# Gated recurrence and maxout feed-forward on one core: two single units first, a split last store, six more transposes by transfer, and a reordered plan

## The chip, the core and the metric

The kernel runs on one core of one Trainium2 chip. The metric is device time in microseconds (us), from the start to the end of one launch. Times are medians over runs; one execution was also taken by the hardware profiler, and its span (first to last instruction) and its own time are given where they are used.

## What is computed

Two stages follow each other. The first is a gated linear recurrence over 768 steps for 4 batches of 8 heads with 48 channels; the second is a feed-forward layer with three gates of which the largest is taken:

```python
for t in range(S):
    state = alpha[:, :, t, :, None] * state + np.einsum('bhd,bhe->bhde', k[:, :, t], v[:, :, t])
    y[:, :, t] = np.einsum('bhd,bhde->bhe', q[:, :, t], state)
...
x = np.ascontiguousarray(attn_out.transpose(0, 2, 1, 3)).reshape(B * S, H * D)
h = np.maximum(np.maximum(x @ w1, x @ w2), x @ w3)
return h @ w_out
```

There are 3072 tokens of width 384 (8 heads x 48) and a hidden width of 768. Inputs and output are float32; the kernel multiplies in float16 and sums in float32.

## The kernel before

**Units.** The work is cut into 24 units: one batch times 128 steps, all 8 heads. Unit u belongs to batch u mod 4 and step block u div 4. Two neighbouring units share one load of alpha, q, k and v (a load number n holds units 2n and 2n+1; a half of it is one unit's 192 KB of one tensor). Loads go into five buffers in turn, on SyncE's queue (SP), line 398.

**First stage, for one unit** (`decay`, `prep`, `output`, `state`). ScalarE (ACT) takes the logarithm of alpha (L498). TensorE (PE) sums it over the steps (L551) and over blocks (L511); ACT exponentiates with both signs (L554, L556). GpSimd (POOL) or VectorE (DVE) multiplies q and k with them (L563), and POOL or ACT scales v (L574, L569). The result, `qk`, is transposed by PE (L533) and left by DVE (L537), or for units from CROSS_IN on it is transposed by a DMA on SP (L581). PE forms scores (L596), DVE masks them (L601), and PE forms the unit's output from scores and from the carried state (L642, L639). ACT scales it into `xb` (L650). PE transposes `xb` (L664) and DVE leaves it as `xT` (L668); for units from CROSS_OUT on a DMA on SP does both (L656), which no unit used before. The state is carried on by PE (L694), DVE (L700) and POOL (L707; DVE in the first block).

**Second stage** (`ffn`). The maximum is rewritten: out = x w1 w_out + max(0, x (w2 - w1), x (w3 - w1)) w_out. So the four weight matrices are loaded once (L428); ACT casts w1 and w_out (L437); DVE forms the two differences `wd` (L446); PE transposes w1 (L463) and multiplies it with w_out (L480) into `w1o`. The matrices are cut in two column parts at WCUTS, and a difference can be formed part by part. Then units pass in pairs: PE multiplies the 256 columns of two units' `xT` with `wd` in pieces of six matmuls (L735), ACT takes the first difference's piece through a rectifier (L746), DVE takes the maximum with the second difference's piece (L751); and PE makes each unit's output of nine matmuls of 384 columns, three with `w1o` and six with w_out (L768). ACT copies it out of PSUM (L779) and issues its store (L780).

**What sets the order.** Every operation is a step of a planner (`Plan`) with an engine, a cost, a rank, and the keys that it reads and writes. `Plan.order` replays the whole kernel with these costs, a model of the DMA queue (`Transfers`) and one of PE's pace (`Clock`): again and again it takes the step that can start first, by rank among equals. The order found is then emitted, and each engine runs its steps in that order. Constants at the top steer it: FIRST is the order of the first loads, EARLY the engines of q, k and v in the units 1 to 11 (a unit that is not named uses POOL for all three), LEAD the lead of a feed-forward's rank over its unit, WARM the filler matmuls on zeros (L676) that were put in after unit 0, PAIRS the unit from which the scores of two units are formed in one step. PSUM's eight banks are handed out by the planner too.

Of the kernel before, what the change touches and what calls it, by code (L numbers as in the profile page):

```python
# [25 lines left out]
QUEUES = ("SP", "POOL")  # L26
DMA_IN = {"SP": 0.9, "POOL": 2.7}
DMA_OUT = {"SP": 0.9, "POOL": 0.9}
DMA_BOTH = {"SP": 0.2, "POOL": 0.85}
# [6 lines left out]
WEIGHTS = ()  # L36
WCUTS = (0, 384, 768)
SUBS = {(1, 0): "DVE", (1, 1): "DVE", (2, 0): "DVE", (2, 1): "DVE"}
FIRST = (("aq", 0, 0, 1), ("aq", 0, 1, 2), ("k", 0, 1, 2), ("w", 0, 0), ("v", 1, 0, 1),
# [5 lines left out]
WARM = (0, 0, 12)  # L45
PAIRS, WIDE = 12, 99
CROSS_IN, CROSS_OUT = 21, 24
FETCH, FETCHES, STORE = 1.0, (24.5, 11.0), 0.3
CLOCK_WINDOW, CLOCK_PHASE, CLOCK_WAKE, CLOCK_KEEP = 3.413, 0.0, 0.75, 0.37
# [71 lines left out]
class Plan:  # L121
# [55 lines left out]
    def order(self):  # L177
        n = len(self.steps)
# [19 lines left out]
        free = dict(dict.fromkeys(HOP, 0.0), SP=SP_FIRST)  # L198
        bank_free = {b: 0.0 for b in range(NBANKS)}
# [19 lines left out]
        while len(seq) < n:  # L219
            best = None  # L220
            for e, cand in pending.items():
                pick = None
                for i in cand:
                    at = self.homes(bank_free, self.steps[i][5])
                    if at is None:
                        continue
                    t = max(ready[i], free[e], at[0])
                    turn = TURN_RANK if e == "PE" and self.steps[i][7] != mode else 0.0
                    key = (t, self.steps[i][2] + turn, i)
                    if pick is None or key < pick:  # L230
                        pick = key
                if pick is not None and (best is None or pick < best[0]):
                    best = (pick, e)
            if best is not None and best[0][0] > fetch:
                dma.store(FETCH)
                fetch += FETCHES[1]
            landing = dma.next()
            if landing and (best is None or landing[0] <= best[0][0]):
                end, i = dma.next(commit=True)
                self.landed[i] = end  # L240
                finish(i, end)
                continue
            (t, _, i), e = best
            _, cost, _, _, _, banks, load, m, late = self.steps[i]
            pending[e].discard(i)
            for k, b in self.homes(bank_free, banks)[1].items():
                place[k] = b
                for j in range(self.width.get(k, 1)):
                    del bank_free[b + j]
            if e == "PE":  # L250
                if m != mode:
                    mode = m
                    cost += TURN_COST
                cost = clock.run(t, cost)
            free[e] = t + cost
            seq.append((t, i))
            if load and e in QUEUES:
                dma.add(e, t + cost + DMA_IN[e], load, i, late)
            else:
                if load:  # L260
                    dma.store(load)
                finish(i, t + cost + HOP[e])
            if i in follows:
                arrive(follows[i], t)
# [5 lines left out]
def kernel(  # L270
# [120 lines left out]

    def load(n, lo, hi, names="aqkv"):
        cb, g = divmod(n, B // UB)
        for x in names:
            t = ld[x][n % 5]

            def run(x=x, t=t):
# [6 lines left out]
                      load=1.82 * (hi - lo) / HG,  # L404
                      late=0.0 if n < 3 else SPARE)

# [3 lines left out]

    def weights(g, gate):
        plan.step("POOL", 0.78, -1.0,
                  lambda: nc.gpsimd.dma_start((w1h, 0, 0, wo16)[g],
                                              matrices[g].rearrange("(t p) f -> p t f", p=P)),
                  reads=[gate], writes=[("w", g, p) for p in range(nparts)], line="weights",
                  load=3.2 if g == 0 else 4.1)
        if g == 0:
            turned()
        else:
            folded()  # L420
# [5 lines left out]
    def wload(g, part):  # L426
        plan.step("SP", 0.5, -1.0,
                  lambda: nc.sync.dma_start(  # L428
                      piece(wst[g], g, part),
                      piece(matrices[g].rearrange("(t p) f -> p t f", p=P), g, part)),  # L430
                  reads=[("ws room", p) for p in casting[0]] if g == 3 else [],
                  writes=[("ws", g, part)], line="loads",
                  load=3.25 * (WCUTS[part + 1] - WCUTS[part]) / DF)
# [8 lines left out]
    def subs(g, part):  # L442
# [4 lines left out]
                      wd[:, :, g - 1, cols], wst[g][:, :, cols], w1h[:, :, cols]),  # L447
                  reads=[("ws", g, part), ("w", 0, part)], writes=[("wd", g, part)])
# [42 lines left out]
    def decay(n):  # L491
# [28 lines left out]
        if cb > 0:  # L520
            m = n - B // UB
            plan.step("DVE", 0.45, 2 * n + 0.5,
                      lambda: nc.vector.tensor_mul(Gs[m % 3], e12s[m % 4][:, :, 1],
                                                   e12s[n % 4][:, :, 0]),
                      reads=[("e", m % 4), ("e", n % 4)], writes=[("G", m % 3)])
# [14 lines left out]
    def prep(u):  # L540
# [12 lines left out]
        plan.step("PE", 0.17, u, cums, banks=[Lk], reads=[("la", n % 3, i)], writes=[Lk])  # L553
# [5 lines left out]
        for w, x, e in ((0, "q", ep), (1, "k", en)):  # L559
# [4 lines left out]
                              qk[:, w, :, :D], ld[x][n % 5][:, hs], e),  # L564
                      reads=[(x, n % 5, i), ("ep" if w == 0 else "en", u % 3)],
# [62 lines left out]
    def output(u):  # L628
# [16 lines left out]
        plan.step("PE", 0.38 if cb else 0.21, u, outs, banks=[yk], writes=[yk],  # L645
# [20 lines left out]
        plan.step("PE", 0.17, u, turn, banks=[xk], reads=[("xb", u % 5)], writes=[xk])  # L666
# [49 lines left out]
    def ffn(f, units):  # L716
# [4 lines left out]
        span = 4 // k  # L721
        npieces = 2 * (NJ // span) + k
        rank = [u0 + LEAD[min(f, 2)] + k * i / npieces for i in range(npieces)]
        for q in range(NJ // span):
            js = range(q * span, (q + 1) * span)
            parts = sorted({p for j in js for p in parts_of(j // 2)})
            for g in range(2):
# [10 lines left out]
                plan.step("PE", 0.656 if span > 1 else 0.643, r, grow, banks=[gk],  # L738
# [5 lines left out]
                if g == 0:  # L744
                    plan.step("ACT", 0.59, r,
# [3 lines left out]
                else:  # L749
                    plan.step("DVE", 0.69, r,  # L750
# [3 lines left out]
        for i in range(k):  # L754
# [5 lines left out]
            parts = [(0, nk)] if m < NU - UB else [(0, nk - 2), (nk - 2, nk)]  # L760
# [21 lines left out]
            plan.step("ACT", 0.86, r, leave, reads=[ok], writes=[("ob room", m % 4)], load=STORE)  # L782
# [13 lines left out]
    for n in range(NU // B):  # L796
        us = list(range(n * B, (n + 1) * B))
        due += [us] if n >= WIDE else [us[:UB], us[UB:]]
    nf = len(due)
    for n in range(NG):  # L800
# [6 lines left out]
        for u in range(n * UB, (n + 1) * UB):  # L807
# [5 lines left out]
            for g, after, x in WEIGHTS:  # L813
                if after == u:
                    weights(g, ("v16", u % 7) if x == "v" else ("qk", u % 7, "qk".index(x)))
# [45 lines left out]
```

## Time and profile before

| What | Value |
|---|---|
| median of three runs | 156.61 us (156.6, 156.61, 157.32) |
| profiled execution, own time | 157.07 us |
| its span, first to last instruction | 155.3 us |
| busy: PE, DVE, ACT, POOL | 138.2, 100.6, 86.5, 67.2 us |
| moved by DMA | 29.45 MB, mean 190 GB/s |

The profile's page lists busy time of each engine, the span in 40 slices, the chain of work that ended last, and groups of instructions by source line. Matmuls overlap each other, so that the duration of one (276 ns on average on L735) is more than the time by which it delays the next; the chain of work shows the latter (six of them take 0.66 us there). In a row of the timeline stand start, duration, engine, line, operation, tiles and the count of merged instructions; in brackets, how long the engine had been idle and what released it.

### The profile page before, as it was taken

What the parts mean: (1) busy time and instruction counts of PE and PEld (TensorE: products, weight loads), DVE (VectorE), ACT (ScalarE), POOL (GpSimd) and SP (SyncE); (2) the same over time, 40 slices, a digit from 0 to 9 for tenths busy, and PEclk for the clock granted to TensorE, in tenths of its full rate; (3) what the DMA queues carried; (4) which work ended last, traced back from release to release, by engine and by line L of the source; (5) the groups of instructions that cost most, each with busy time, mean ns of one, the idle gap of its engine ahead of it and who ended that gap; (6) DMA issues with size and microseconds to landing.
All of it is one profiled execution on the core that took longest, in us unless ns stands there. A gap on an engine that the chain in (4) does not pass through costs nothing.

```text
span 155.3 us, 4013 instructions
## 1 busy us (share of the span) xinstructions
PE 138.2 (89%) x1600; PEld 105.8 (68%) x1600; DVE 100.6 (65%) x171; ACT 86.5 (56%) x173; POOL 67.2 (43%) x95
## 2 busy tenths in 40 slices
PE   0578537999998999999999999999999999999990
PEld 0244425757777967798778688878797787868750
DVE  7044756398599997669768869958684752923220
ACT  3734707747547666496768284848575462535221
POOL 0332190011912154076999749999858600000000
PEclk9999999999999999999999999999999999999999
DMA  6999999999999999999999999999894232011202
GB/s 123 227 240 253 325 209 344 330 181 232 207 243 219 180 239 246 211 269 189 231 219 207 222 253 231 180 243 267 195 202 86 101 72 77 24 55 51 83 18 101
DMA packets 109394, 29.45 MB, mean 190 GB/s; under 512 B 103104, under 2 KB 109376, under 8 KB 109376
## 3 DMA queue, kind: packets, MB, share of 16 engines
q1 hardware_dynamic: 105632, 24.38, 75.4%
q10 hardware_dynamic: 3744, 4.82, 9.1%
q8 instruction: 12, 0.20, 0.5%
q14 instruction: 6, 0.05, 0.1%
HBM read 23.69 MB, written 4.72 MB: 183 GB/s over the span
## 4 chain that ended last, share of the span: by engine, by line
PE 76%; SPq 6%; issue 4%; DVE 4%; DMA 3%; POOL 2%; ACT 2%; ACTq 0%; POOLq 0%
PE psum L735 30%; PE psum L768 23%; PE psum L533 5%; SPq L398 5%; PE psum L596 4%; DMA qn<-in_q_dram 3%; PE psum L642 3%; PE psum L639 2%; POOL qk L563 2%; PE psum L551 2%; PE psum L664 2%; PE psum L480 2%; PE psum L694 2%; DVE LA L601 2%; SPq L428 1%
## 5 line engine op out<-in xcount | busy, mean ns | idle before, releaser
L735 PE MATMUL psum<-xT,wd 128*128 128x256 f16 x432 | 55.7, 276 | 0.2
L735 PEld LDWEIGHTS <-wd 128*128 128x128 f16 x432 | 41.0, 99 | 7.1 <-issue 0.5
L563 POOL TENSOR_TENSOR qk<-qn,ep 128x384 f16<-128x384 f32 x21 | 21.5, 1028 | 37.5 <-ACT ep L554 29.7
L751 DVE TENSOR_TENSOR hT<-psum,hT 128x512 f16<-128x512 f32 x36 | 24.2, 686 | 16.0 <-PE psum L735 12.1
L601 DVE TENSOR_TENSOR LA<-psum,c 128x1024 f16<-128x1024 f32 x24 | 28.6, 1216 | 7.0 <-PE psum L596 7.0
L746 ACT ACTIVATE hT<-psum 128x512 f16<-128x512 f32 x36 | 21.5, 605 | 17.2 <-PE psum L735 16.9
L768 PE MATMUL psum<-wo,hT 128*128 128x384 f16 x144 | 27.3, 326 | 0.0
L779 ACT COPY ob<-psum 128x384 f32<-128x384 f32 x24 | 11.5, 478 | 23.2 <-PE psum L768 22.8
L768 PEld LDWEIGHTS <-hT 128*128 128x128 f16 x144 | 14.1, 98 | 9.3
L650 ACT ACTIVATE xb<-psum,c 128x384 f16<-128x384 f32 x24 | 13.9, 582 | 10.7 <-PE psum L642 9.6
L574 POOL TENSOR_SCALAR v<-vn,c 128x384 f16<-128x384 f32 x21 | 12.6, 601 | 13.7 <-DMA vn<-in_v_dram 13.5
L563 POOL TENSOR_TENSOR qk<-kn,en 128x384 f16<-128x384 f32 x17 | 18.4, 1087 | 0.2 <-DMA kn<-in_k_dram 0.2
L537 DVE COPY qkT<-psum 128x1024 f16<-128x1024 f16 x21 | 14.2, 685 | 5.7 <-PE psum L533 5.0
L533 PE MATMUL psum<-c,qk 128*128 128x128 f16 x168 | 14.5, 232 | 3.8 <-POOL qk L563 3.7
L707 POOL TENSOR_TENSOR Z<-U,G 48x192 f16<-48x192 f32 x32 | 15.7, 504 | 3.9 <-DVE U L700 2.8
L768 PE MATMUL psum<-w1o,xT 128*128 128x384 f16 x72 | 15.7, 326 | 0.0
L533 PEld LDWEIGHTS <-qk 128*128 128x128 f16 x168 | 11.2, 104 | 5.7 <-POOL qk L563 4.6
L554 ACT ACTIVATE ep<-psum 128x384 f32<-128x384 f32 x24 | 11.9, 495 | 2.8 <-PE psum L551 2.7
L668 DVE COPY xT<-psum 128x384 f16<-128x384 f16 x24 | 8.3, 352 | 7.7 <-PE psum L664 6.5
L551 PE MATMUL psum<-la,c 128*128 128x384 f16 x24 | 8.5, 354 | 4.5 <-ACT la L498 4.5
L498 ACT ACTIVATE la<-an 128x768 f16<-128x768 f32 (+1 forms) x15 | 10.7, 711 | 2.8 <-DMA an<-in_alpha_dram 1.4
L556 ACT ACTIVATE en<-psum 128x384 f32<-128x384 f32 x24 | 12.0, 501 | 0.0
(40 smaller groups left out, 155.0 us busy)
## 6 DMA issues: line engine op xcount, KB each, us to landing
out_dram<-ob ACTq DMA_DIRECT2D x24, 192.0 KB, 3.0
ws<-in_moe_w_dram SPq DMA_DIRECT2D x6, 576.0 KB, 5.9
an<-in_alpha_dram SPq DMA_DIRECT2D x9, 384.0 KB, 6.1
qn<-in_q_dram SPq DMA_DIRECT2D x9, 384.0 KB, 6.1
kn<-in_k_dram SPq DMA_DIRECT2D x9, 384.0 KB, 5.3
vn<-in_v_dram SPq DMA_DIRECT2D x9, 384.0 KB, 5.8
an<-in_alpha_dram SPq DMA_DIRECT2D x6, 192.0 KB, 4.6
qn<-in_q_dram SPq DMA_DIRECT2D x6, 192.0 KB, 4.2
```

The source lines that it names most:

```text
L533: nc.tensor.transpose(live[tk][:, w, j, :], qk[:, w, 2 * j:2 * j + 2, :], ident)
L537: plan.step("DVE", 0.69, u, lambda: nc.vector.tensor_copy(out=qkT, in_=live[tk]), reads=[tk], writes=[("qkT", u % 3)])
L556: plan.step("ACT", 0.49, u, lambda: nc.scalar.activation(out=en, in_=live[Lk], func=AFT.Exp, scale=-1.0), reads=[Lk], writes=[("en", u % 3)])
L563: nc.gpsimd if eng == "POOL" else nc.vector).tensor_mul(
L574: lambda: nc.gpsimd.tensor_scalar(out=v16, in0=ld["v"][n % 5][:, hs], scalar1=vsc, scalar2=1.0, op0=AOP.mult, op1=AOP.mult),
L601: lambda: nc.vector.tensor_mul(LA.rearrange("p a b t -> p (a b) t"), live[Ak].rearrange("p a (b t) -> p (a b) t", t=P), maskA.unsqueeze(1) ...
L650: lambda: nc.scalar.activation(out=xb, in_=live[yk].rearrange("p a b -> p (a b)"), func=AFT.Copy, scale=ysc),
L707: eng.tensor_mul(Zn[rows, :, cols], U[rows, :, cols], G[rows, i * NP:(i + 1) * NP].unsqueeze(2).broadcast_to([D, NP, D]))
L735: nc.tensor.matmul(live[gk][:, jj, :], wd[:, kt, g, j * P:(j + 1) * P], xT[:, kt, :], start=(kt == 0), stop=(kt == NFT - 1))
L746: lambda h=h, gk=gk: nc.scalar.activation(out=h, in_=live[gk], func=AFT.Relu),
L751: lambda h=h, gk=gk: nc.vector.tensor_max(h, live[gk], h),
L768: nc.tensor.matmul(live[ok], a[:, i * P:(i + 1) * P], w, start=(kt == 0), stop=(kt == nk - 1))
```

## The change

- `SINGLE = 2`: the units 0 and 1 go through `ffn` each by itself. A piece is then nine matmuls of 128 columns (three hidden blocks of 128; `span` is 3 for one unit and 2 for a pair), and there are eight of them for the two units in place of six of 256 columns. `LAST = 0` leaves the end in pairs.
- The last unit's output is left by two engines: ACT copies the left 192 columns and stores them on its own queue, DVE copies the right 192 columns and SP stores them.
- `CROSS_OUT` goes from 24 to 18: for the units 18 to 23 a DMA on SP transposes `xb`; the PE transposes (L664) and the DVE copies (L668) of these six are gone. `CROSS_IN` goes from 21 to 22: unit 21's `qk` is transposed by PE and left by DVE again.
- `PAIRS` goes from 12 to 10: units 10 and 11 form their scores in one step.
- `WARM` has a count of 0: no filler matmuls.
- `FIRST`, `EARLY`, `LEAD` and `WCUTS` have new values: unit 0's v, q and alpha come first; the weight parts are two thirds and one third of the columns; DVE multiplies for units 0, 1, 3, 4, 6, 9 and 11 and ACT scales v of units 1, 6, 9 and 10. The number of multiplications on DVE stays ten.
- The planner's replay gets two more rules: POOL steps and certain DVE steps (flag `mode`) exclude each other in time (`held`), and no more than six SP transfers may be open (`lanes`). Some costs change by a few hundredths. The model's second queue is ACT's in place of POOL's, but the weights are still loaded on SP (`WQUEUE = "SP"`). The unused function `weights` is gone.

```diff
-LEAD = (6.0, 9.0, 7.0)
-EARLY = {1: ("POOL", "DVE", "POOL"), 3: ("DVE", "DVE", "POOL"), 4: ("POOL", "POOL", "POOL"),
-         5: ("DVE", "POOL", "POOL"), 6: ("DVE", "DVE", "POOL"), 7: ("POOL", "DVE", "POOL"),
-         8: ("POOL", "DVE", "ACT"), 9: ("POOL", "DVE", "ACT"), 10: ("POOL", "DVE", "ACT"),
-         11: ("POOL", "POOL", "POOL")}
-WCUTS = (0, 384, 768)
+LANES, LANES_USED, LANDING = {"SP": 6, "ACT": 99}, 2, 2.4
+LEAD = (4.0, 7.0, 2.0, 7.0)
+EARLY = {0: ("DVE", "POOL", "POOL"), 1: ("DVE", "POOL", "ACT"), 3: ("DVE", "DVE", "POOL"),
+         4: ("DVE", "POOL", "POOL"), 5: ("POOL", "POOL", "POOL"), 6: ("DVE", "DVE", "ACT"),
+         7: ("POOL", "POOL", "POOL"), 8: ("POOL", "POOL", "POOL"), 9: ("DVE", "DVE", "ACT"),
+         10: ("POOL", "POOL", "ACT"), 11: ("DVE", "POOL", "POOL")}
+WCUTS = (0, 512, 768)
-FIRST = (("aq", 0, 0, 1), ("aq", 0, 1, 2), ("k", 0, 1, 2), ("w", 0, 0), ("v", 1, 0, 1),
-         ("k", 0, 0, 1), ("k", 1, 0, 1), ("w", 0, 1), ("qa", 1, 0, 1), ("w", 1, 1),
-         ("w", 1, 0), ("v", 0, 0, 1), ("v", 0, 1, 2), ("k", 1, 1, 2), ("a", 1, 1, 2),
-         ("w", 3, 1), ("q", 1, 1, 2), ("w", 3, 0), ("w", 2, 0), ("v", 1, 1, 2), ("w", 2, 1),
-         ("aqkv", 2, 0, 2), ("a", 3, 0, 1), ("a", 3, 1, 2), ("qk", 3, 0, 1), ("v", 3, 0, 1),
-         ("k", 3, 1, 2), ("q", 3, 1, 2), ("v", 3, 1, 2))
-WARM = (0, 0, 12)
-PAIRS, WIDE = 12, 99
-CROSS_IN, CROSS_OUT = 21, 24
+FIRST = (("v", 0, 0, 1), ("qa", 0, 0, 1), ("k", 0, 1, 2), ("a", 0, 1, 2), ("k", 1, 0, 1),
+         ("q", 0, 1, 2), ("w", 0, 0), ("a", 1, 0, 1), ("k", 0, 0, 1), ("v", 1, 0, 1),
+         ("k", 1, 1, 2), ("w", 0, 1), ("v", 0, 1, 2), ("w", 1, 0), ("w", 1, 1), ("w", 3, 1),
+         ("aq", 1, 1, 2), ("q", 1, 0, 1), ("w", 3, 0), ("w", 2, 0), ("w", 2, 1),
+         ("v", 1, 1, 2), ("aqkv", 2, 0, 2), ("k", 3, 0, 1), ("a", 3, 0, 2), ("vq", 3, 0, 1),
+         ("kv", 3, 1, 2), ("q", 3, 1, 2))
+WARM = (1, 0, 0)
+BACK, WQUEUE, WTAX = 2, "SP", 0.1
+SINGLE, LAST = 2, 0
+PAIRS, WIDE = 10, 99
+CROSS_IN, CROSS_OUT = 22, 18
...
+                    if e == "POOL" or e == "DVE" and self.steps[i][7]:
+                        t = max(t, held["DVE" if e == "POOL" else "POOL"])
+                    if self.steps[i][6] and len(lanes) >= LANES[e]:
+                        if lanes[-LANES[e]] is None:
+                            continue
+                        t = max(t, lanes[-LANES[e]])
...
-        span = 4 // k
+        span = (3, 2, 0, 1)[k - 1]
...
-            parts = [(0, nk)] if m < NU - UB else [(0, nk - 2), (nk - 2, nk)]
+            parts = [(0, nk)] if m < NU - UB else [(0, nk - span), (nk - span, nk)]
...
-            plan.step("ACT", 0.86, r, leave, reads=[ok], writes=[("ob room", m % 4)], load=STORE)
+            if m < NU - 1:
+                plan.step("ACT", 0.86, r, leave, reads=[ok], writes=[("ob room", m % 4)], load=-STORE)
+                continue
+            left, right = slice(0, DM // 2), slice(DM // 2, DM)
+            rows = out[b * S + cb * P:b * S + (cb + 1) * P, :]
+
+            def leave_left(m=m, ok=ok, rows=rows):
+                nc.scalar.copy(out=obs[m % 4][:, left], in_=live[ok][:, left])
+                nc.scalar.dma_start(rows[:, left], obs[m % 4][:, left])
+
+            plan.step("ACT", 0.7, r, leave_left, reads=[ok], writes=[("ob room", m % 4)],
+                      load=-STORE)
+            plan.step("DVE", 0.3, r,
+                      lambda m=m, ok=ok: nc.vector.tensor_copy(out=obs[m % 4][:, right],
+                                                               in_=live[ok][:, right]),
+                      reads=[ok], writes=["right"])
+            plan.step("SP", 0.4, r,
+                      lambda m=m, rows=rows: nc.sync.dma_start(rows[:, right],
+                                                               obs[m % 4][:, right]),
+                      reads=["right"], writes=["done"], load=-STORE)
...
+    due = [x for us in due for x in ([[u] for u in us] if us[0] < SINGLE or us[0] >= NU - LAST
+                                     else [us])]
```

More of the change, by code (lines that the diff above doesn't have):

```diff
@@ L239, in order @@
                 end, i = dma.next(commit=True)
+                lanes[number[i]] = end
                 self.landed[i] = end
@@ L426, in wload @@
     def wload(g, part):
[L427 to L428 removed]
+        room = [("ws room", p) for p in casting[0]] if g == 3 else []
+        gate = [asked[-1 - BACK]] if len(asked) > BACK and WQUEUE == "ACT" else []
+        plan.step(WQUEUE, 0.5, -1.0,
+                  lambda: (nc.scalar if WQUEUE == "ACT" else nc.sync).dma_start(
                       piece(wst[g], g, part),
                       piece(matrices[g].rearrange("(t p) f -> p t f", p=P), g, part)),
[L431 to L433 removed]
+                  reads=gate + room, writes=[("ws", g, part)],
+                  line="weights" if WQUEUE == "ACT" else "loads",
+                  load=3.25 * (WCUTS[part + 1] - WCUTS[part]) / DF
+                  + (WTAX if WQUEUE == "SP" else 0.0))
         if g in (0, 3):
```

63 lines of the change are left out of this document (30 added, 33 removed).

## The prediction, on record before the result

> **What bounds the kernel now.** I read the page's busy shares first, then the windows of five microseconds, then PE's own timeline at the start, and the chain of work at both ends. The page's first part and its slices:
>
> ```profile
> PE 138.2 (89%) x1600; PEld 105.8 (68%) x1600; DVE 100.6 (65%) x171; ACT 86.5 (56%) x173; POOL 67.2 (43%) x95
> ...
> PE   0578537999998999999999999999999999999990
> ```
>
> PE is the busiest engine, and its slices are full from the eighth on (27 us). What it loses lies ahead of that. The windows (duration; busy time and count of PE, PEld, DVE, ACT, POOL; granted clock; DMA share and GB/s):
>
> ```profile
> 10.00:15.00 5.00, 3.99 (x28) 2.19 (x26) 1.77 (x2) 2.32 (x3) 1.58 (x2) 1.00 0.96 234
> 15.00:20.00 5.00, 2.33 (x21) 1.65 (x21) 3.59 (x5) 3.66 (x6) 1.27 (x1) 1.00 1.02 301
> 20.00:25.00 5.00, 2.80 (x35) 2.10 (x36) 2.74 (x3) 1.10 (x2) 3.52 (x4) 1.00 1.16 247
> 25.00:30.00 5.00, 4.49 (x44) 3.26 (x41) 2.02 (x5) 3.92 (x8) 0.00 (x0) 1.00 1.10 335
> 30.00:35.00 5.00, 4.72 (x49) 2.93 (x47) 4.51 (x6) 2.80 (x5) 0.59 (x1) 1.00 0.95 217
> 45.00:50.00 5.00, 4.71 (x80) 3.62 (x80) 4.85 (x9) 3.75 (x9) 1.16 (x2) 1.00 1.11 225
> ```
>
> So there are three ways to a shorter time: less PE work behind 27 us, more of it done before, and a shorter end. PE's timeline at the start of the feed-forward:
>
> ```profile
> 26.11 0.49 PE L664 MATMUL psum<-c,xb 128*128 128x128 f16 x3
> ...
> 27.05 2.62 PE L735 MATMUL psum<-xT,wd 128*128 128x256 f16 x12
> 29.51 0.33 PE L664 MATMUL psum<-c,xb 128*128 128x128 f16 x3
> 29.68 0.82 PE L735 MATMUL psum<-xT,wd 128*128 128x256 f16 x6
> ...
> 33.78 0.82 PE L735 MATMUL psum<-xT,wd 128*128 128x256 f16 x6
> ...
> 34.81 1.14 PE L480 MATMUL psum<-wo,w1T 128*128 128x384 f16 x6
> ```
>
> Two things are to be seen. The same three transposes take 0.49 us at 26.11 and 0.33 us at 29.51, and twelve of L735 take 2.62 us where later six go on in 0.66: PE works at half pace until about 29.4, although the granted clock is 1.00 throughout. And the piece at 33.78 is the first that needs the last matrix, moe_w3.
>
> **The change part by part.**
>
> *PE work.* These rows of the chain are the time by which a block of matmuls delays what follows, at full pace:
>
> ```profile
> 42.52 0.45 PE psum L533 x8
> 42.97 0.66 PE psum L735 x6
> ...
> 44.73 0.33 PE psum L596 x8
> ...
> 66.71 0.17 PE psum L664 x3
> ...
> 103.85 0.55 PE psum L596 x16
> ```
>
> Six units' L664 go: 6 x 0.17 = 1.02 us less. Unit 21's L533 comes back: 0.45 more. Units 10 and 11 join their scores: 2 x 0.33 against 0.55, 0.11 less. The two single units need 8 pieces of nine 128-column matmuls at 0.45/8 = 0.056 us each, 4.03 us, against 6 x 0.66 = 3.96, so 0.07 more. Sum: -0.61 us, all of it in stretches where PE is full. The work that goes along on DVE (six copies of L668 less, one L537 more) and ACT (four copies out of PSUM for three) lies beside PE there and is put at nothing; DVE is busy for 65% of the span.
>
> The filler matmuls cost nothing now, since they ran between 6.8 and 13.3 us, where PE waited for data; their removal brings nothing either. They did not change the pace: the work behind them was still slow.
>
> *The start.* Why does the feed-forward begin only at 27.05? It needs `xT` of both units 0 and 1. POOL and DVE ahead of it:
>
> ```profile
> 18.73 1.60 POOL L563 TENSOR_TENSOR qk<-qn,ep 128x384 f16<-128x384 f32 x1 [6.16 <-ACT ep L554]
> 20.29 2.10 POOL L563 TENSOR_TENSOR qk<-kn,en 128x384 f16<-128x384 f32 x1
> 22.38 1.14 POOL L574 TENSOR_SCALAR v<-vn,c 128x384 f16<-128x384 f32 x2
> ```
>
> ```profile
> 18.12 1.36 DVE L446 TENSOR_TENSOR wd<-ws,w1h 128x1152 f16<-128x1152 f32 x1 [0.45 <-DMA ws<-in_moe_w_dram]
> 19.73 1.81 DVE L446 TENSOR_TENSOR wd<-ws,w1h 128x1152 f16<-128x1152 f32 x1 [0.25 <-DMA ws<-in_moe_w_dram]
> ...
> 31.80 1.60 DVE L446 TENSOR_TENSOR wd<-ws,w1h 128x1152 f16<-128x1152 f32 x1
> 33.33 1.21 DVE L601 TENSOR_TENSOR LA<-psum,c 128x1024 f16<-128x1024 f32 x1
> 34.46 1.34 DVE L446 TENSOR_TENSOR wd<-ws,w1h 128x1152 f16<-128x1152 f32 x1
> ```
>
> The first difference was there at 21.54 (19.73 + 1.81), yet v of units 0 and 1 was scaled at 22.38 only, loaded late and queued on POOL behind two multiplications of unit 2. Those took 1.60 and 2.10 us while DVE formed the difference; the page's mean of that kind is 1.03 us:
>
> ```profile
> L563 POOL TENSOR_TENSOR qk<-qn,ep 128x384 f16<-128x384 f32 x21 | 21.5, 1028 | 37.5 <-ACT ep L554 29.7
> ```
>
> The Trainium skill ("SBUF — State Buffer", on its two separate sides) says that GpSimd and a two-input VectorE operation lock each other out of a shared port pair; the 2.10 us agrees. By that rule ten multiplications left on DVE, now also in units 0 and 1, block POOL just the same and the start would gain less; the planner's new rule places them apart, and the sum below has room for both.
>
> With the change v of unit 0 is the first transfer and v of unit 1 is ahead of moe_w2, so the wait moves to moe_w2. Its last part comes behind 12 half-unit loads where it came behind 10: 2 x 0.197 MB at some 250 GB/s (the windows) are 1.6 us, so the first difference is complete near 23.1, its first two thirds near 22.3. Feed-forward then starts near 22.5, one unit at a time, about 4.5 us sooner.
>
> That is not the gain, because moe_w3 is next. It is behind 15 half-unit loads where it was behind 16, so it lands 0.8 us sooner:
>
> ```profile
> 24.95 1.10 SPq L428 DMA_DIRECT2D ws<-in_moe_w_dram  x1
> ```
>
> ```profile
> DMA to landing us min/median/max: 4.9/5.9/8.2
> ```
>
> The first row is SP's timeline, the second what the view of line 428 says of all weight loads. Issued at 24.95, the last part was there by about 33.1 at the latest. Now it would be 32.3, with the two-thirds part 1.6 us earlier (0.39 MB), at 30.7; its difference takes 1.34 x 4/3 = 1.8 us, so the first piece with it can run at 32.5 in place of 33.78, 1.3 us sooner. What PE had left over at 33.78 of work that does not need moe_w3 is one L480 group (0.98 us by three such pieces) and unit 3's output; with PE fed from 22.5 on, the L480 group can be done before. Upper bound of the gain: 1.3 + 0.98 = 2.3 us. Lower bound: 0, if PE is idle for as long as it was early. After 33 us nothing stands in the way for some ten microseconds: both units' second differences and outputs, then units 2 and 3, are 2.1 + 2.9 + 3.9 + 2.9 us of PE work. I take 1.4 us, somewhat above the middle, because the last part's difference (a third, 0.9 us) ends near 33.4 where it ended at 35.80, and the half pace should end with the denser work sooner than 29.4.
>
> *The order behind.* All of it is found anew. PE's only loss there that shows is 0.29 us of idle time in the 45 to 50 window. I put it at nothing. The bounds are -0.6 us (this and the 0.28 of the 30 to 35 window both gone) and +1.5 (three new losses as large as the 0.51 of the 25 to 30 window), nearest to the many full windows.
>
> *The end.* ACT's timeline and the two groups that a half-width copy lies between:
>
> ```profile
> 151.54 0.34 ACTq L780 DMA_DIRECT2D out_dram<-ob  x1
> 151.98 0.48 ACT L779 COPY ob<-psum 128x384 f32<-128x384 f32 x1 [0.47 <-ACT ob L779]
> 152.49 0.34 ACTq L780 DMA_DIRECT2D out_dram<-ob  x1
> ```
>
> ```profile
> L517 ACT ACTIVATE e<-psum,c 128x16 f32<-128x16 f32 x12 | 3.4, 283 | 0.6 <-PE psum L511 0.6
> ```
>
> ACT still copies and issues unit 22 first; its last copy falls from 0.48 to about 0.38 us (halfway to the 0.283 of 16 columns). So the left half is issued 0.1 us sooner. DVE's half does not wait for unit 22's copy and is issued before. I take -0.1, with 0 to -0.4 for the smaller last transfer.
>
> *Transposes by transfer.*
>
> ```profile
> L581 SPq DMA_TRANSPOSE qkT<-qk x3: 1232/1232/1332, 114.2 to 124.1; - x3
> ...
> DMA to landing us min/median/max: 3.1/4.4/4.7
> ```
>
> ```profile
> 135.69 0.58 ACT L650 ACTIVATE xb<-psum,c 128x384 f16<-128x384 f32 x1 [0.45 <-PE psum L642]
> ```
>
> ```profile
> 138.76 4.09 PE L735 MATMUL psum<-xT,wd 128*128 128x256 f16 x36
> ```
>
> ```profile
> 109.58 1.43 SPq L398 DMA_DIRECT2D vn<-in_v_dram  x1
> ```
>
> The last load leaves SP at 111.0, so the six transposes of `xb` have SP to themselves, with two of `qk`. The tightest is unit 23: its `xb` is there at 136.27, and its pair's first piece is the last third of the 36 matmuls, at about 141.5. A transfer issued at 136.3 lands 3.1 to 4.7 us later, at 139.4 to 141.0. It is hidden, by 0.5 us at worst.
>
> **Sum.** -0.6 (PE work) - 1.4 (start) - 0.1 (end) = -2.1 us. On the profiled execution, 157.07 us of which 155.3 are span, that is 155.0. It lies 0.46 above the median of the runs shown; on the median of 156.61 it is 154.5 us, my forecast.
>
> **The rivals.**
>
> *The start gives nothing.* PE is early with the single units but waits for moe_w3 all the same. For it: moe_w3 gains only 0.8 us of transfers. Against: the L480 group was left over. Then -0.7 us: 155.9.
>
> *The transposes are late.* Units 22 and 23 queue on SP; 1.23 us of issue and 4.7 us of landing behind 136.3 give 142.2, 0.7 after the need, and PE, with 0.6 us less to do, comes 0.6 sooner still. PE idles 1.3 us: -2.1 + 1.3 is 155.8. For it: the landing of 4.7. Against: the plan can put the other pair's work between.
>
> *The half pace lasts: slower.* PE ran at half pace while it was busy for 2.33 to 3.99 of 5 us, and changed where it was busy for 4.49. With fillers gone, and moe_w3 and w_out both due near 30, PE may do the single units by 27 and starve until 33. Then the 7 us from 29.4 to 36.4 run at half pace and cost 3.5 us; with -0.7 for the rest and about -1 for the earlier single units that is +1.8: 158.4. It decides where PE's busy time between 25 and 35 stays under some 4 of each 5 us. The Trainium skill ("TensorE: Matmul & The Clock Gate", Part 1) has the rule: full rate comes after a busy window of about 3.4 us and is lost after an idle one. The trace agrees with the first half (dense from 27.05, fast by 29.5); it has no idle stretch that shows the second.
>
> **How the numbers follow.** The forecast, 152.6 to 155.7, has a chance of 0.62: its best end is -0.6 - 2.3 - 0.4 - 0.6 = -3.9. The start that gives nothing has 0.16, late transposes 0.08, the half pace 0.14. The range leaves out the half pace and the last mishaps: 152.6 to 157.0. A measurement can tell about 0.5% (0.8 us) from no change. Faster (below 155.83) holds the forecast and a little of the second and third case, 0.64; same holds most of these two, 0.2; slower 0.16.
>
> **What would show it.** The profile after should have L735 of 128 columns start near 22.5, the first piece with moe_w3's difference near 32.5, L664 with 54 matmuls, no L676, and PE full from there. The order behind gives no idle window over 0.5 us. The transposes' landing shows in a wait of L735 near 140. It is wrong if the matmuls past 30 us still take twice their time, or if new waits of PE on POOL or DVE stand between 35 and 110.

## The result, and the profile after

| | before | with the change |
|---|---|---|
| median, first measurement | 156.55 us (20 runs, 155.61 to 157.32) | 154.69 us (20 runs, 153.0 to 158.26) |
| ratio, 95% interval | 1 | 0.9863 [0.9835, 0.9891] |
| ratio over three measurements | 1 | 0.9866 [0.9845, 0.9887] |
| profiled execution, own time (span) | 157.07 (155.3) | 156.54 (154.8); a second one 154.31 (152.5) |

The change makes the kernel faster by 1.34%, 2.1 us; 154.5 was predicted. (The ratios leave out runs over 1.5% above the fastest of their kernel, 11 of the change's 32; with all 32 its median is 0.988 of before's, 1.9 us less, and its mean 0.991, 1.4 us less.) The first profiled execution lies 1.85 us above its median. So the kernel was profiled again, unaltered (experiment `again`), and that one lies 0.35 below the median. Both are shown, since they differ in something that matters.

The pages' first part and the slices, first profile, then second:

```profile
span 154.8 us, 4044 instructions
...
PE 134.0 (87%) x1614; PEld 105.0 (68%) x1614; DVE 97.4 (63%) x168; ACT 86.9 (56%) x174; POOL 65.2 (42%) x94
...
PE   0143739789999999999999999999999999999990
...
PEclk9999975859999999999999999999999999999999
```

```profile
span 152.5 us, 4044 instructions
...
PE   0143849699999999999999999999999999999990
...
PEclk9999975899999999999999999999999999999999
```

PE is still full from some 30 us to the end. In the slices from 19 to 35 us lies the difference between the two: the granted clock falls twice in the first profile and once in the second. The windows that answer to those of before, second profile:

```profile
20.00:25.00 5.00, 3.56 (x43) 2.95 (x39) 3.16 (x4) 3.37 (x8) 0.00 (x0) 0.60 1.11 250
25.00:30.00 5.00, 4.19 (x51) 3.50 (x50) 3.67 (x5) 2.87 (x7) 1.34 (x1) 0.71 1.01 351
30.00:35.00 5.00, 4.29 (x47) 3.12 (x47) 4.37 (x5) 3.06 (x6) 0.98 (x1) 1.00 1.05 206
45.00:50.00 5.00, 5.00 (x63) 3.52 (x61) 2.45 (x5) 2.86 (x7) 0.58 (x1) 1.00 0.98 209
```

PE does more from 20 to 25 us than before (3.56 us for 2.80), 0.73 less from 25 to 35 (busy time tells little there, since half the rate doubles it), and the 0.29 us lost between 45 and 50 are gone. Most of these were one wait for DVE, in PE's timeline of before:

```profile
49.96 0.40 PE L596 MATMUL psum<-qkT 48*128 48x128 f16 x8 [0.26 <-DVE qkT L537]
```

DVE was busy for 4.85 of these 5 us then, and is for 2.45 in the second profile. PE's timeline at the start of the feed-forward, second profile (L748 is the old L735, L492 the old L480):

```profile
22.49 2.08 PE L748 MATMUL psum<-xT,wd 128*128 128x128 f16 x18 [0.69 <-DVE xT L681]
...
24.89 2.13 PE L748 MATMUL psum<-xT,wd 128*128 128x128 f16 x18
...
30.70 1.14 PE L492 MATMUL psum<-wo,w1T 128*128 128x384 f16 x6 [0.80 <-ACT wo L448]
31.68 0.36 PE L655 MATMUL psum<-v,LA 128*128 128x48 f16 x8
31.88 2.11 PE L492 MATMUL psum<-wo,w1T 128*128 128x384 f16 x12
33.83 0.33 PE L677 MATMUL psum<-c,xb 128*128 128x128 f16 x3
34.00 1.67 PE L748 MATMUL psum<-xT,wd 128*128 128x128 f16 x27
```

The single units begin at 22.49, as forecast, in 128 columns. But the first piece with moe_w3's difference is the one at 34.00, not at 32.5. All three L492 groups stand ahead of it in PE's order, and the first of them waited for w_out's cast (ACT's timeline, second profile):

```profile
29.18 1.47 ACT L448 CAST wo<-ws 128x1536 f16<-128x1536 f32 x1 [1.63 <-DMA ws<-in_moe_w_out_dram]
```

The end, in ACT's, DVE's and SP's timelines of the second profile:

```profile
149.05 0.34 ACTq L793 DMA_DIRECT2D out_dram<-ob  x1
149.49 0.32 ACT L802 COPY ob<-psum 128x192 f32<-128x192 f32 x1 [0.47 <-DVE ob L808]
149.84 0.34 ACTq L803 DMA_DIRECT2D out_dram<-ob  x1
```

```profile
148.87 0.36 DVE L808 COPY ob<-psum 128x192 f32<-128x192 f32 x1 [2.17 <-PE psum L781]
```

```profile
149.29 0.36 SPq L812 DMA_DIRECT2D out_dram<-ob  x1
```

DVE has copied the right half and SP has begun to issue its store before ACT starts the left one, and the left copy takes 0.32 us where the whole one took 0.48.

**Where the time came from.** I counted each matmul at the interval by which it delays the next at full pace (0.162 us for 384 columns, 0.109 for 256, 0.056 for 128, some 0.04 for one of the scores), and summed what was still to be done at several times. That is a working of mine from the traces, not a view:

| PE work left, us | before | first profile | second profile |
|---|---|---|---|
| in all | 125.22 | 124.77 | 124.77 |
| at 32 us | 116.66 | 116.52 | 115.51 |
| at 36 us | 112.93 | 114.05 | 111.51 |
| at 40 us | 108.97 | 110.00 | 107.55 |
| at 50 us | 100.01 | 100.17 | 97.72 |
| at 110 us | 40.91 | 40.81 | 38.58 |

Second profile against before: 0.45 us less to do; at 40 us 1.42 ahead, so 0.97 from the start; at 50 us 2.29 ahead, so 0.87 between 40 and 50. From there to 110 us the lead stays, and the span is 2.76 us shorter, of which the end has about 0.3. The profiled pair flatters the change: the ratio gives 2.1 us. And the 0.97 from the start are this execution's; other executions of the same start stand below, where the prediction is gone through.

### The profile page after: what moved, and what is told of

It reads as the page before. It is cut to its first block, busy times and chain, and to the rows that moved or that the text cites. A ratio compares the mean times of both kernels' runs of the same rounds, so it can differ in the third digit from the quotient of the medians.

```text
span 154.8 us, 4044 instructions
## 1 busy us (share of the span) xinstructions
PE 134.0 (87%) x1614; PEld 105.0 (68%) x1614; DVE 97.4 (63%) x168; ACT 86.9 (56%) x174; POOL 65.2 (42%) x94
## 4 chain that ended last, share of the span: by engine, by line
PE 77%; SPq 11%; DMA 7%; ACT 2%; issue 1%; ACTq 0%
PE psum L748 30%; PE psum L781 23%; SPq L416 10%; PE psum L545 5%; DMA ws<-in_moe_w_out_dram 4%; PE psum L609 4%; PE psum L492 3%; PE psum L655 3%; DMA ws<-in_moe_w_dram 3%; PE psum L563 2%; PE psum L652 2%; PE psum L707 2%; PE psum L677 2%; PE psum L523 1%; ACT wo L448 1%; SPq L438 1%
## 5 line engine op out<-in xcount | busy, mean ns | idle before, releaser
L748 PE MATMUL psum<-xT,wd 128*128 128x256 f16 (+1 forms) x468 | 55.5, 272 | 1.4 <-DVE xT L681 1.4
L748 PEld LDWEIGHTS <-wd 128*128 128x128 f16 x468 | 43.2, 102 | 6.9 <-DVE wd L457 1.4
L764 DVE TENSOR_TENSOR hT<-psum,hT 128x512 f16<-128x512 f32 (+1 forms) x37 | 24.5, 674 | 14.1 <-PE psum L748 11.9
L759 ACT ACTIVATE hT<-psum 128x512 f16<-128x512 f32 (+1 forms) x37 | 21.3, 591 | 16.4 <-PE psum L748 15.5
L575 POOL TENSOR_TENSOR qk<-qn,ep 128x384 f16<-128x384 f32 x17 | 16.9, 996 | 25.5 <-ACT ep L566 7.9
L575 POOL TENSOR_TENSOR qk<-kn,en 128x384 f16<-128x384 f32 x21 | 21.2, 1016 | 9.1 <-ACT en L568 5.7
L792 ACT COPY ob<-psum 128x384 f32<-128x384 f32 x23 | 11.0, 479 | 21.6 <-PE psum L781 19.7
L587 POOL TENSOR_SCALAR v<-vn,c 128x384 f16<-128x384 f32 x20 | 12.1, 608 | 15.8 <-DMA vn<-in_v_dram 7.6
L549 DVE COPY qkT<-psum 128x1024 f16<-128x1024 f16 x22 | 14.9, 686 | 4.1 <-PE psum L545 3.9
L663 ACT ACTIVATE xb<-psum,c 128x384 f16<-128x384 f32 x24 | 13.7, 583 | 5.6 <-PE psum L655 2.4
L655 PE MATMUL psum<-v,LA 128*128 128x48 f16 x192 | 11.0, 185 | 0.7 <-ACT v L582 0.7
```

The lines of the kernel that those rows point to most:

```text
L549: plan.step("DVE", 0.69, u, lambda: nc.vector.tensor_copy(out=qkT, in_=live[tk]), reads=[tk], writes=[("qkT", u % 3)])
L575: nc.gpsimd if eng == "POOL" else nc.vector).tensor_mul(
L655: nc.tensor.matmul(yp[:, 2 * j + p, :], LA[:, p, j, :], v16[:, 2 * j + p, :], start=(cb == 0), stop=True, skip_group_check=True)
L663: lambda: nc.scalar.activation(out=xb, in_=live[yk].rearrange("p a b -> p (a b)"), func=AFT.Copy, scale=ysc),
L748: nc.tensor.matmul(live[gk][:, jj, :], wd[:, kt, g, j * P:(j + 1) * P], xT[:, kt, :], start=(kt == 0), stop=(kt == NFT - 1))
L759: lambda h=h, gk=gk: nc.scalar.activation(out=h, in_=live[gk], func=AFT.Relu),
```

## The experiments

Differences against the change are differences of ratios times 156.6 us; their intervals hold those of both.

**again**: the change unaltered.

> The changed kernel once more, unaltered, for a second profile of its start. In its first profile TensorE was granted full rate from 18.0 to 21.4 us, half of it from 21.4 to 28.2, full to 31.7, half to 35.1 and full from there. If the pace at the start is a matter of when a 3.4 us stretch happens to begin, this profile shows other turning points, and a span other than 154.8 us by up to about 2 us; if the order of the work sets it, the same turning points within 0.5 us.

Ratio 0.9858 [0.9806, 0.9910], own time of the profiled execution 154.31. The rate turns at 17.63, 21.05 and 27.87 us where it turned at 18.00, 21.41 and 28.24, within 0.4 us; but the second fall, at 31.65, did not come. And the order of the work alone doesn't set the turns: with the same order on PE the first turn on record is a rise at 29.37 us in `undo_cross`, at 28.01 in `cross14` and at 29.82 in `cross16`. The second profile's view of the transposes by transfer (L669), and of the PE transposes left (L677):

```profile
L669 SPq DMA_TRANSPOSE xT<-xb x6: 1180/1524/2207, 113.7 to 132.4; - x6
...
DMA to landing us min/median/max: 2.3/3.5/3.8
```

```profile
L677 PE MATMUL psum<-c,xb x54: 217/219/315, 20.8 to 104.8; 128*128 128x128 f16 x54
```

54 are left of 72, and no wait of PE hangs on a transfer: the views of waits of both profiles list none of PE's from 35 us to the end.

**undo_cross**: the transposes as before.

```diff
-CROSS_IN, CROSS_OUT = 22, 18
+CROSS_IN, CROSS_OUT = 21, 24
```

> The change with CROSS_IN, CROSS_OUT back at 21, 24; its TensorE order is the changed kernel's for the first three quarters. My account (TensorE is full there, so six transposes of 0.17 us less and one of 0.45 more are the gain): 0.57 us slower than the change. Rival (transfers only shift the wait to the end of the kernel): the same time as the change, or less.

Ratio 0.9922 [0.9891, 0.9953]: 0.9 (+-0.6) us of the gain gone, where the PE work alone is 0.57. The interval takes in both; the 0.3 us over may be the wait that the last pair has here, or two of 0.28 and 0.18 us at 104.33 and 110.12 us. PE's timeline has the first:

```profile
140.99 1.47 PE L748 MATMUL psum<-xT,wd 128*128 128x256 f16 x12 [0.30 <-DVE xT L681]
```

**undo_head**: the start as before (loads, engines, leads, weight parts, fillers, pairs from the first unit on). Cut to its core:

```diff
-WCUTS = (0, 512, 768)
+WCUTS = (0, 384, 768)
...
-WARM = (1, 0, 0)
+WARM = (0, 0, 12)
...
-SINGLE, LAST = 2, 0
+SINGLE, LAST = 0, 0
```

> The change with FIRST, EARLY, LEAD, WCUTS, WARM and pairs at the start as before; what stays is the transposes by transfer, PAIRS at 10, the split last store and the planner's two new rules. My account (start worth 1.4 us, the rest 0.7): 1.4 us slower than the change and 0.7 faster than before. Rival (the start gives nothing, the rest all): as fast as the change.

Ratio 0.9926 [0.9894, 0.9958]: 0.94 (+-0.6) us slower than the change, 1.2 faster than before. So the start's settings together are worth about 0.9, less than the 1.4 predicted, though 1.4 is inside the interval. The window of 45 to 50 us is full here, but PE waits for DVE some 6 us later, behind a window in which DVE was busy for 4.86 of 5 us (the windows, then PE's timeline):

```profile
45.00:50.00 5.00, 5.00 (x83) 4.63 (x80) 4.19 (x10) 4.27 (x10) 1.59 (x2) 1.00 1.03 195
50.00:55.00 5.00, 4.95 (x67) 4.04 (x65) 4.86 (x11) 2.62 (x6) 0.58 (x1) 1.00 0.95 188
55.00:60.00 5.00, 4.63 (x55) 3.28 (x56) 4.31 (x10) 3.59 (x10) 1.97 (x3) 1.00 1.20 230
```

```profile
55.71 0.40 PE L609 MATMUL psum<-qkT 48*128 48x128 f16 x8 [0.28 <-DVE hT L764]
```

So the stall has moved, and it isn't gone. By the count of work above, PE loses 1.3 us between 40 and 60 us here (20 us less the work done in them), 1.4 in before, and 0.5 in the second profile of the change.

Its nine runs scatter by 0.55 us (standard deviation), those of the change by 1.5 (32 runs).

**fill60**: fillers on zeros wherever PE waits at the start, to have full rate for all that follows.

```diff
-WARM = (1, 0, 0)
+WARM = (1, 0, 60)
```

> The change with 60 filler matmuls on zeros that the planner puts wherever TensorE would be idle from unit 1 on (about 10 to 33 us). If half pace between 21 and 35 us costs the change a part of its gain, the fillers keep the full pace from about 20 us on, the profile shows no half pace behind 25 us, and the time falls by 1 to 2 us with less scatter. If the pace is not what limits the start, the fillers get in the way of the work and the time is the same or up to 1 us longer.

Ratio 1.0167 [1.0126, 1.0208]: 4.7 us slower than the change. The fillers did what they were put in for: the trace has full rate from 20.54 us on, without a fall to the end of PE's work. About half of the price is in PE's timeline at the start:

```profile
17.41 3.50 PE L689 MATMUL psum<-Z 128*128 128x384 f16 x11
20.84 0.40 PE L609 MATMUL psum<-qkT 48*128 48x128 f16 x8
...
33.05 1.14 PE L492 MATMUL psum<-wo,w1T 128*128 128x384 f16 x6
```

Eleven fillers take 3.5 us in front of the scores at 20.84, which began at 17.84 in `again`. They stand ahead of these scores in PE's order, so the first units' chain is 3 us late, and by 40 us PE has done 2.3 us less work than in `again`. The other half is lost between 50 and 60 us, where PE waits for DVE (0.60 us at 53.49, 0.58 at 55.91) in an order that was found anew. So this run prices the fillers together with another order.

**pairs_first** and **pairs_lead**: the rest of the change's start, but pairs from the first unit on. They differ in the leads; the second has those of before.

```diff
-LEAD = (4.0, 7.0, 2.0, 7.0)
+LEAD = (4.0, 2.0, 7.0)
...
-SINGLE, LAST = 2, 0
+SINGLE, LAST = 0, 0
```

> The change with all units in pairs (SINGLE 0; LEAD 4, 2, 7), first loads, engines and cuts as changed. If the single units carry the gain of the start (their pieces fill 22 to 28 us): slower than the change by about 1 us, and the profile shows the first feed-forward piece near 25 us and less useful TensorE work done by 32 us. If the new order of loads carries it: the same as the change within 0.4 us.

Ratio 1.0143 [1.0099, 1.0188]. It can't be read as a price of pairs: PE has new waits that end at 54.3, 62.4, 63.5, 95.9 and 113.9 us, far from the start. The order of the whole came out badly; only the leads differ from the next run. So the second was made:

```diff
-LEAD = (4.0, 7.0, 2.0, 7.0)
+LEAD = (6.0, 9.0, 7.0)
...
-SINGLE, LAST = 2, 0
+SINGLE, LAST = 0, 0
```

> The change with all units in pairs and the leads of before (6, 9, 7), first loads, engines and cuts as changed. If the single units carry the start: useful TensorE work done by 32 us falls from 9.3 to about 7.5 us as in the other kernel with pairs, and the time is 1 to 2 us longer than the change. If that other kernel was slow through its leads alone: the same time as the change within 0.5 us.

Ratio 0.9926 [0.9895, 0.9956], 0.94 (+-0.6) us slower than the change: as much as undoing the whole start. PE's timeline shows where:

```profile
25.75 1.44 PE L748 MATMUL psum<-xT,wd 128*128 128x256 f16 x6 [3.29 <-DVE xT L681]
```

The first piece comes at 25.75 in place of 22.49. About 1.1 us of that are the wait for unit 1's `xT`; the rest is moe_w2, whose first difference began at 22.54 in this execution and at 20.41 in `again`. So the whole 0.94 can't be put down to the pairs. A fairer neighbour is the profile of `undo_split` below, with single units and the first difference at 22.40: it has done 8.2 us of work by 32 us and 16.2 by 40, against 7.8 and 15.4 here. (The rate rose at 28.48 there and at 30.21 here, which is part of this.)

**undo_split**: ACT leaves the last output alone.

```diff
-            if m < NU - 1:
+            if m < NU:
```

> The change with the last unit's output left by ScalarE alone, as before. The time from the start of the last matmul to the end of the span was 4.3 us before and 4.0 in the two profiles of the change. If the split is the reason, it is 4.3 again and the time 0.3 us longer, which the times alone can hardly tell; if it stays 4.0, something else shortened the end.

Ratio 0.9908 [0.9870, 0.9946], 0.66 (+-0.7) us slower: the time alone doesn't settle it. The rows do. ACT's and PE's timelines:

```profile
151.43 0.48 ACT L792 COPY ob<-psum 128x384 f32<-128x384 f32 x1 [0.49 <-ACT ob L792]
151.94 0.34 ACTq L793 DMA_DIRECT2D out_dram<-ob  x1
```

```profile
149.29 1.46 PE L781 MATMUL psum<-wo,hT 128*128 128x384 f16 x8
```

From the last matmul's end (149.29 + 1.46) to the end of the span (154.87) there are 4.12 us; in before 3.97, in the change's two profiles 3.67 and 3.70. The split is worth 0.3 (against before) to 0.4 us (against this run).

**fill_fold**: six fillers ahead of the first L492 product, written into its own PSUM bank, against a second fall of the rate.

```diff
+                zero = Zs[1][0].rearrange("p a b -> p (a b)")
+                for _ in range(6 if kt == 0 else 0):
+                    nc.tensor.matmul(live[key], zero[:, :P], zero, start=True, stop=True)
```

> The change with six filler matmuls on zeros at one place alone: just ahead of the first product of w1 with w_out, where TensorE waited 0.8 to 1.4 us for the cast of w_out in the two profiles. If the loss of full rate at about 31.6 us (one of the two profiles) is what makes single executions up to 2 us longer, these fillers keep it: the slow half of the times moves down, median 0.3 to 1 us shorter than the change. If the half pace there is not set by such a short idle stretch, the time is the same or 0.4 longer (what the fillers take).

Ratio 0.9872 [0.9820, 0.9924] from six runs: not to be told from the change. Whether the second fall can be had away cheaply stays open.

**cross14** and **cross16**: more units turned by transfer. (`CROSS_OUT = 14`, then 16.)

```diff
-CROSS_IN, CROSS_OUT = 22, 18
+CROSS_IN, CROSS_OUT = 22, 14
```

> The change with transposes by transfer from unit 14 on in place of 18: 0.67 us of TensorE work less. My account (TensorE bounds that stretch): 0.7 us faster than the change, if SyncE's queue, where loads of the last units now stand behind transposes that wait for their unit, does not delay a load past its use. Rival: that wait delays the loads; then TensorE shows idle windows between 95 and 120 us and the time is the same or longer.

Ratio 1.0323 [1.0286, 1.0359], 7.2 us slower than the change. SP's timeline, then the windows:

```profile
112.00 1.98 SPq L416 DMA_DIRECT2D vn<-in_v_dram  x1
114.07 9.94 SPq L669 DMA_TRANSPOSE xT<-xb  x6
```

```profile
110.00:115.00 5.00, 3.40 (x55) 1.94 (x50) 3.36 (x4) 3.34 (x8) 4.69 (x8) 0.83 1.17 259
115.00:120.00 5.00, 3.89 (x52) 2.91 (x52) 3.03 (x4) 1.09 (x3) 4.43 (x8) 0.50 0.63 124
120.00:125.00 5.00, 5.00 (x34) 3.85 (x32) 2.00 (x4) 2.32 (x5) 4.16 (x7) 0.64 0.39 79
```

SP issues all its loads first and then six transposes in a row, the first at 114.07. The `xT` of units 14 and 15 come then only, PE has no feed-forward to put between, idles for 2.7 us in two windows, and loses full rate from 113.35 to 123.59: in the third window it is busy all the time and does 34 matmuls.

```diff
-CROSS_IN, CROSS_OUT = 22, 18
+CROSS_IN, CROSS_OUT = 22, 16
```

> The change with transposes by transfer from unit 16 on. If from unit 16 on no load of SyncE still stands behind a waiting transpose: 0.33 us faster than the change. If it does, as from unit 14 on: idle windows of TensorE between 105 and 120 us, half pace behind them, and several us longer.

Ratio 0.9883 [0.9850, 0.9915], as the change within its interval; the 0.33 us of PE work can't be seen. But its start, the same code as in `again`, shows what the start hangs on. PE's timeline:

```profile
25.90 2.08 PE L748 MATMUL psum<-xT,wd 128*128 128x128 f16 x18 [3.46 <-DVE xT L681]
```

**again2**: the change unaltered, beside before_cross, pairs_lead and cross16 on one chip.

> The changed kernel unaltered, a third time, so that its neighbours here have it on the same chip. Time against before as in the first two measurements, ratio 0.986. In its profile the first feed-forward piece between 22.5 and 24.5 us, by when moe_w2 lands (21.4 to 23.5 so far), and a half pace that ends near 28 us or near 35 us; the span is about 152.5 in the first case and 2 us more in the second.

Ratio 0.9878 [0.9839, 0.9917], six runs from 154.98 to 159.07. In its profile the first feed-forward piece starts at 22.82 and the half pace ends at 27.01 us, as expected for the good case; the span is 153.2 all the same. PE has a wait here that neither of the first two profiles has, 0.68 us at 89.22 for an `xb` from ACT (L663).

**before_cross**: the kernel before, with the change's transposes alone.

```diff
-CROSS_IN, CROSS_OUT = 21, 24
+CROSS_IN, CROSS_OUT = 22, 18
```

> The kernel before with CROSS_IN, CROSS_OUT at 22, 18 alone; its TensorE order is that of before for the first three quarters. My account: 0.57 us faster than before (0.9964), all of it between 115 and 150 us. Rival (transfers cost nothing or bring nothing at the end without the rest of the change): within 0.2 us of before.

Ratio 0.9986 [0.9960, 1.0012]: 0.2 us, between 0.6 faster and 0.2 slower. The 0.57 us of PE work is just inside. The stall of before is still there:

```profile
45.00:50.00 5.00, 4.58 (x82) 3.54 (x81) 4.86 (x10) 3.74 (x9) 2.17 (x2) 1.00 1.00 197
```

## Why the prediction was right, point by point

Its sum was -2.1 us, and -2.1 was measured. Some of that is luck: the start brought less than its term, the order behind brought what was put at nothing, and the two nearly cancel. (The lower end of its range, 152.6, is 0.1 below its own sum of -3.9.)

*PE work, -0.61.* The mechanism is right (54 L677, two batches of scores joined), the size by my count of matmuls 0.45: the joined scores are the same 16 matmuls, so their 0.11 isn't in it, and the single units cost 0.11 more in place of 0.07. That it is hidden elsewhere for DVE, ACT and SP is right too: landings of 2.3 to 3.8 us (second profile) as in the sum, no wait of PE behind them. Undoing it costs 0.9 (+-0.6), doing it alone brings 0.2 (-0.2 to 0.6). Both agree with 0.45; neither is sharp.

*Start, -1.4: mis-sized, and not steady.* It is 0.97 in the second profile. The first half of the step held there: v first, feed-forward near 22.5. What failed is "the first piece with it can run at 32.5 in place of 33.78". I had looked at moe_w3 alone. In PE's order the L492 groups come before that piece, and they need two thirds of w_out, cast at 29.18 + 1.47 = 30.65 us. The old first group started at 31.40, so what moved up is 0.7 us, not 1.3. Having an L480 group "done before" could not be, for the same reason. And the 0.7 is not to be counted on: seven of the profiles have the changed start with the same order on PE (up to 93 us at least), and the first L492 group began between 30.29 (`again2`) and 33.51 us (`cross16`) in those read for it. The count of work says what such differences do, one profile each:

| PE, us | work done by 40 us | lost from 40 to 60 us |
|---|---|---|
| before, before_cross, undo_head (old start) | 16.2, 16.9, 16.4 | 1.4, 1.4, 1.3 |
| first profile, again, again2, undo_cross, undo_split, cross14, cross16 | 14.7, 17.2, 17.6, 16.7, 16.2, 15.5, 14.4 | 0.4, 0.5, 0.5, 0.5, 0.7, 0.5, 0.4 |
| pairs_lead | 15.4 | 0.5 |

The seven have done 16.1 us of work by 40 us on the average, no more than before. So the start itself is ahead in good executions alone. The 0.94 (+-0.6) of `undo_head` looks like the 0.97, but need not be the same gain: its profile loses 0.8 us more than `again` between 40 and 60 us.

*The order behind, at nothing: wrong by 0.9 us.* The bound of -0.6 was too narrow because I took PE's visible idle time (0.29 us) for the loss, while the work done tells 0.87. The share "DVE is busy for 65% of the span" hid that DVE was full just ahead of this wait (4.85 of 5 us). The third column shows with what the loss goes: with the old start, under the new rules and pairs (`undo_head`) as under the old ones (`before_cross`). It is small with the changed first loads, engines of q, k and v, weight parts and no fillers, also when the leads and the first pairs are those of before (`pairs_lead`); `pairs_first` and `fill60`, whose orders went wrong elsewhere too, lose 1.3 and 2.8. Which of these four settings does it was not tried singly, nor the changed start under the old rules; since PE waits for a full DVE, the engines are the likeliest, but that is argued and not shown.

*End, -0.1.* Right in its mechanism, 0.3 in size, within its bound of -0.4. The copy fell by 0.16, to 0.32 us; that the other 0.1 or so comes from a last transfer half as large is argued, no run has it alone.

*Rival "the half pace lasts".* Its mechanism took place, in single executions. The first profile has it, in windows cut where the trace's clock record turns:

```profile
18.00:21.41 3.41, 1.73 (x33) 1.15 (x31) 1.37 (x2) 3.40 (x6) 0.00 (x0) 1.00 1.03 362
21.41:24.82 3.41, 1.98 (x18) 1.81 (x19) 3.02 (x4) 1.38 (x3) 0.00 (x0) 0.50 1.01 218
24.82:28.24 3.42, 3.42 (x39) 3.25 (x38) 1.03 (x2) 2.54 (x7) 0.99 (x1) 0.50 0.93 269
28.24:31.65 3.41, 1.64 (x30) 1.21 (x29) 2.42 (x3) 1.64 (x2) 0.00 (x0) 1.00 1.10 357
31.65:35.07 3.42, 3.42 (x19) 1.73 (x19) 2.97 (x3) 0.96 (x2) 0.97 (x1) 0.50 0.91 160
```

From 28.24 PE waits for w_out and is busy for 1.64 of 3.41 us; the next window is at half rate, and the L492 groups run in it. The table of work left shows the price: 1.01 us behind the second profile at 32 us, 2.54 at 36. The sign that the prediction gave for being wrong, matmuls past 30 us at twice their time, is there in this execution: the first six of L492 take 2.04 us at 31.57, and 1.14 in the second profile. The rival gave 3.5 us for a fall over 7 us; it lasted 3.4, and the execution that had it, at 156.54 us, was still faster than the one of before, at 157.07.

*Rival "the start gives nothing":* not so for the start's settings as a whole, by `undo_head`. But in its own terms, PE early and then waiting all the same, it is not refuted: the seven profiles are not ahead at 40 us on the average. *Rival "the transposes are late":* not so with six. With ten it happens at once, by another way than I gave: it isn't the transposes that queue on each other behind 136 us, but all of them behind the last loads.

**What stays open** is which of the start's settings took away the stall, and how much of the change's scatter comes from its start. For the start speak three rows of the first difference (L457) in the same code, from DVE's timelines of `again`, the first profile and `cross16`:

```profile
20.41 1.76 DVE L457 TENSOR_TENSOR wd<-ws,w1h 128x1536 f16<-128x1536 f32 x1 [0.84 <-DMA ws<-in_moe_w_dram]
```

```profile
21.27 1.76 DVE L457 TENSOR_TENSOR wd<-ws,w1h 128x1536 f16<-128x1536 f32 x1 [1.61 <-DMA ws<-in_moe_w_dram]
```

```profile
23.83 1.76 DVE L457 TENSOR_TENSOR wd<-ws,w1h 128x1536 f16<-128x1536 f32 x1 [3.76 <-DMA ws<-in_moe_w_dram]
```

Each waited for moe_w2's landing, and the first feed-forward piece followed 2.07 to 2.08 us later in all three. Before, it waited for v on POOL; now it waits for a transfer whose landing differed by 3.4 us between these three executions, and on that hangs where PE's gap falls against the rate's windows. Over the seven profiles the work done by 40 us falls as this row starts later: 17.2 us of it with 20.41, 17.6 with 20.75 (`again2`), 16.7 with 21.55 (`undo_cross`), 16.2 with 22.40 (`undo_split`), 15.5 with 22.57 (`cross14`), 14.4 with 23.83; only the first profile, with its second fall of the rate, is off that line (14.7 with 21.27). The old start in the new kernel scatters less. No run holds moe_w2's landing fixed, so this is a relation, not a test.

## What to carry to other kernels

When a start is made earlier, list every input that the next dozen instructions of the bottleneck engine's queue need, in that queue's order: the gain ends at the latest of them (here w_out), not at the one that the feature is about. Judge an engine's loss by work left at given times: here 0.29 us of visible idle time went with 0.87 us of lost work. Compare it over several executions before a lead is called a gain. When a stall is gone from its window, look whether it stands in the next one. Filling gaps with dummy work did not pay here, where real work was delayed behind it.

## What the runs showed of the hardware

- The granted rate changed in steps of about 3.41 us (3.41, 6.83, 3.41 and 3.42 us between the turns of the first profile; 10.24 in `cross14`). It rose after a window that PE filled, and fell after windows that were not idle: PE was busy for 1.73 and 1.64 of 3.41 us in those shown above. In the second profile two windows kept it, one with a little more and, at the end, one with less. So the busy time of a window does not decide it alone, and what does is not shown:

```profile
27.87:31.28 3.41, 2.07 (x32) 1.44 (x30) 2.50 (x4) 1.47 (x1) 0.00 (x0) 1.00 1.12 348
147.34:150.75 3.41, 1.49 (x10) 0.69 (x7) 0.36 (x1) 0.80 (x2) 0.00 (x0) 1.00 0.25 84
```

- The Trainium skill ("TensorE: Matmul & The Clock Gate", Part 1) puts the loss of full rate behind an idle window of about 3.4 us. The step agrees; the condition is narrower than what these rows show, where the rate was lost behind windows with 1.73 and 1.64 us of work.
- The column of the granted clock reads 1.00 until the trace's first record of a turn, which in before is at 29.44 us. So 1.00 at the start of the profile before was no proof of full rate; the duration of the same three transposes showed the half rate (0.49 against 0.33 us).
- A transpose of 128 x 384 in float16 by transfer held SP for 1.18 to 2.21 us (second profile), and six of them in a row for 9.94 (`cross14`).
